# Zeros between the real products of the head of a sinkhorn-attention and MLP kernel

## The chip, the cores and the metric

One core of a Trainium2 chip runs the whole program. The metric is the device time of one execution in microseconds; the kernel before was run three times, and its median is the figure to compare with. The profile is one further execution, taken by the hardware profiler; its span runs from the first to the last instruction and is shorter than the time of a run. Engines: PE is TensorE's matmul, PEld its weight load, DVE VectorE, ACT ScalarE, POOL GpSimd, SP SyncE.

## The reference

Attention over sorted blocks (batch 4, 8 heads, sequence 768, head size 64, 8 blocks of 96), then an MLP over 3072 tokens with 512 columns inside and 2048 hidden.

```python
P = sort_net
for _ in range(5):
    P = np.exp(P - P.max(-1, keepdims=True))
    P = P / (P.sum(-1, keepdims=True) + 1e-09)
    P = P / (P.sum(-2, keepdims=True) + 1e-09)
k_sorted = einsum('bhij,bhjcd->bhicd', P, k_blocks)   # v alike
scores = scale * q_b @ k_sb.T
attn = softmax(scores)          # within each block
x = (attn @ v_sb)               # then as (tokens, 512)
h = x @ w_in
out = (h * cos(h)) @ w_out
```

## The kernel before

The order of every engine's instructions is the order of the Python code: the scheduling is manual, and each engine works through its own queue in order. The pools only hand out buffers, and waits are set between the instructions that share one.

The work is cut into eight pieces n of 384 tokens (four blocks, u = 0 to 3, of one batch half). For a piece: `qk` makes scores in PSUM (`sc`), takes the maximum and subtracts it on VectorE (`mx`, `s`); `expo` makes the exponentials on ScalarE (`p_buf`); `p_transpose` turns them on TensorE (`pps`) and copies them to `pT`; `av` multiplies with the sorted values `vS` and normalizes on VectorE (`r`, `xn`); `x_transpose` turns the result (`xps`) into `xT`. `moe_up` makes h (line 553), its cosine (ScalarE, line 557) and the product `gg` (VectorE, line 560); `moe_down` makes the output (line 570). While one piece is in its MLP, slots between its products carry the attention of the next.

The head comes before the first `moe_up`:

- Loads: `sort_net` at once; then q, k and v of the first batch on POOL's queue (lines 195 to 197), the weights later.
- `keep_warm(n)` (line 216) takes a tile `idle` of the pool `big` and issues n products of zeros, 256 columns wide, from the tile `warm`. `keep_warm(16)` is TensorE's first work.
- The normalization rounds: `product` (line 252) sums over columns on TensorE, one `sk` for each of the two groups g of batches; between them ScalarE makes `E` (line 313), VectorE `rr`, `T`, `ci` (lines 332 to 335). One round over rows first, then four rounds `it`. Rounds 1 and 2 also carry sixteen transposes of q (`qps`, line 294), whose copy to `q_turned` ScalarE makes a round later. The last round ends in `bd` (line 274), the matrices that sort k and v.
- `v_turn` (line 405) makes `bdv` from `bd`, copied by ScalarE.
- `k_sort_0` (line 349), four calls: 16, 16, 8 and 8 products `ks` of 32 columns; the first and third are cast to `kTs` by VectorE, the second and fourth by ScalarE, four casts for each call.
- `v_next` (line 605), eight calls here: each makes eight products `vs` (line 422, 64 columns) and one copy to `vS` on ScalarE. The first two take their tile from `big`, the later ones from `acc`.
- In between stand `qk(0, 0)` to `qk(0, 3)`, the four `expo`, the first two `p_transpose`, `av` and `x_transpose`. The first score needs all casts of `kTs` of this part.

PSUM: pool `big` has three buffers of two banks (1024 fp32 columns), pool `acc` two buffers of one bank (512 columns). A tile in a buffer that was used before waits until the last reader of the old tile is done.

Of the kernel before, what the change touches and what calls it, by code (L numbers as in the profile page):

```python
# [18 lines left out]
def kernel(  # L19
# [15 lines left out]
    nc = tc.nc  # L35
# [177 lines left out]
    early = const.tile([128, 1], FP32, name="early")  # L213
    nc.scalar.activation(early[:], half_pi[:], AF.Exp)

    def keep_warm(times):

        idle = big.tile([128, 256], FP32, name="idle", tag="big")
        for _ in range(times):
            nc.tensor.matmul(  # L220
                idle[:], warm[:], warm[:, :1].to_broadcast([128, 256]), start=True, stop=True)

    keep_warm(16)

# [24 lines left out]
    def along(t):  # L249
        return t[:].unsqueeze(1).to_broadcast([128, 2 * H, nb])  # L250

    def product(lhs, rhs):
        ps = acc.tile([128, nb], FP32, name="sk", tag="acc")
        nc.tensor.matmul(
            ps[:], lhs.rearrange("p x j -> p (x j)"), rhs[:], start=True, stop=True)
        return ps

    for g in range(NG):
        nc.vector.reciprocal(ci[g][:], cs[g][:])
        nc.vector.scalar_tensor_tensor(  # L260
            L[g][:], rows_of, ci[g][:], along(E[g]), op0=ALU.mult, op1=ALU.mult)
    sk = [product(L[g], maskj) for g in range(NG)]
    keep_warm(3)
    nc.vector.tensor_copy(same[:], rows_of)
    nc.vector.tensor_copy(
# [20 lines left out]
    def q_turn(n, z, pool, tag):  # L286

        ps = pool.tile([128, 2, IC, QR, blk // QR], BF16, name="qps", tag=tag)  # L290
        for e in range(2):
            for hp in range(2):
                for r in range(QR):
                    nc.tensor.transpose(
                        ps[hp * D:(hp + 1) * D, e, :, r],
                        q_rows[:, (z * 2 + e) * 2 + hp, r * D:(r + 1) * D], ident[:blk, :blk])

        def place(hp, rows):
            dst = q_of(n, hp)[rows, :QW].rearrange("d (i h c) -> d h i c", h=H2, c=blk)
            return dst[:, z * 2:z * 2 + 2], ps[rows].rearrange("d e i r p -> d e i (r p)")  # L300

        if n == 0:
            return [place(0, slice(0, 128))]
        return [place(hp, slice(hp * D, (hp + 1) * D)) for hp in range(2)]
# [6 lines left out]
    for it in range(4):  # L311
        for g in range(NG):
            nc.scalar.activation(E[g][:], T[g][:], AF.Exp, scale=ci[g][:])
        if it > 1:
            copy_on(A, *turned[0])
        sk = [product(same, E[g]) for g in range(NG)]
        if it in (1, 2):
            turned = q_turn(0, it - 1, big, "big")
        keep_warm((3, 0, 0, 3)[it])
        if it == 1:  # L320

            nc.gpsimd.tensor_copy(held[:], cs[1][:])
            for z in range(3):
                load_w_in(z)
            v_permute(slice(0, 64), D // 2, False)
        elif it == 2:
            load_w_in(3)
            load_q(1)
            for z in range(4):
                load_w_out(z)  # L330
        for g in range(NG):
            nc.vector.reciprocal(rr[g][:], sk[g][:])
            nc.vector.tensor_tensor_reduce(
                T[g][:], E[g][:], rr[g][:], 1.0, 1e-9, ALU.mult, ALU.add, cs[g][:])
            nc.vector.reciprocal(ci[g][:], cs[g][:])
            if it == 3:
                spread(g)
# [10 lines left out]

    def k_sort_0(ih, t0, nt, eng, pool, tag):

        ps = pool.tile([128, nt, 2 * MH], FP32, name="ks", tag=tag)
        for t in range(nt):
            k_products(ps, t, t0 + t, slice(64, 128),
                       bds[0][64:, H:, ih * IC:(ih + 1) * IC])
        ms, ts = slice(ih * MH, (ih + 1) * MH), slice(t0, t0 + nt)
        psv = ps.rearrange("p t (e m) -> p e m t", e=2)
        for hp in range(2):
            for x in range(2):
                copy_on(eng, kT[0][hp * D:(hp + 1) * D, hp + x, ms, ts],
                        psv[x * D:(x + 1) * D, hp])  # L360

    def k_sort_1(t0, eng, pool, tag):
        ps = pool.tile([128, 8, 2 * NB], FP32, name="ks", tag=tag)
        for t in range(8):
            k_products(ps, t, t0 + t, slice(0, 128),
                       bds[0][:, :H].rearrange("p x i -> p (x i)"))
        copy_on(eng, kT[1][:, ::2, :, t0:t0 + 8], ps.rearrange("p t (e m) -> p e m t", e=2))

    def k_sort_g(t0, eng, pool, tag):
        ps = pool.tile([128, 4, 4 * NB], FP32, name="ks", tag=tag)  # L370
        for t in range(4):
            k_products(ps, t, t0 + t, slice(0, 128), bds[1].rearrange("p x i -> p (x i)"),
                       pair)
        copy_on(
            eng, kT2[:, ::2, :, :, t0:t0 + 4].rearrange("p e b m t -> p b e m t"),
            ps.rearrange("p t (b e m) -> p b e m t", b=2, e=2))
# [26 lines left out]
    bdv = const.tile([128, 2 * H, nb], BF16, name="bdv")  # L403

    def v_turn():
        ps = big.tile([128, 128], FP32, name="bdp", tag="big")
        for r in (0, 64):
            nc.tensor.matmul(
                ps[r:r + 64], ident[:, 64 - r:128 - r], bds[0].rearrange("p x i -> p (x i)"),
                start=True, stop=True)  # L410
        nc.scalar.copy(bdv.rearrange("p x i -> p (x i)"), ps[:])
# [2 lines left out]
        return vperm[:, d * blk:d * blk + 128] if permuted else vv[:, d]  # L414

    def v_sort_b(b, d0, nd, eng, pool, tag):
        ps = pool.tile([128, nd, 2 * NB], FP32, name="vs", tag=tag)


        rows, xs = slice(0, 64 + b * 64), slice((1 - b) * H, (2 - b) * H)  # L420
        for t in range(nd):
            nc.tensor.matmul(  # L422
                ps[:, t], v_cols(d0 + t, b == 1 or d0 + t >= D // 2)[rows],
                bdv[rows, xs].rearrange("p x i -> p (x i)"), start=True, stop=True)
        copy_on(
            eng, vS[0][:, b * 2 * NB:(b + 1) * 2 * NB, d0:d0 + nd],
            ps[:blk].rearrange("p t n -> p n t"))

    def v_sort_g(d0, nd, eng, pool, tag):
        ps = pool.tile([128, nd, 4 * NB], FP32, name="vs", tag=tag)  # L430
        for t in range(nd):
            nc.tensor.matmul(  # L432
                ps[:, t], v_cols(d0 + t, True), bds[1].rearrange("p x i -> p (x i)"),
                start=True, stop=True)
        copy_on(eng, vS[1][:, :, d0:d0 + nd], ps[:blk].rearrange("p t n -> p n t"))
# [9 lines left out]

    def qk_part(n, u, part, pool, tag):
        w = len(part)
        sc = pool.tile([128, w, 512], FP32, name="sc", tag=tag)
        for h2 in range(H2):
            for e, hp in enumerate(part):  # L450
                scores(sc[:, e, h2 * blk:(h2 + 1) * blk], n, u, h2, hp)
        scv = sc[:blk, :, :H2 * blk].rearrange("p e (h c) -> p e h c", c=blk)
        mx = small.tile([blk, w, H2], FP32, name="mx", tag="mx")
        nc.vector.reduce_max(mx[:], scv, axis=AX.X)  # L454
        nc.vector.tensor_tensor(  # L455
            s_t[n, u][:, part[0]:part[0] + w], scv, mx.to_broadcast([blk, w, H2, blk]),
            op=ALU.subtract)
# [40 lines left out]

    def p_transpose(n, u, eng, pool, tag):
        p = pb.pop((n, u))  # L500
        ps = pool.tile([128, 2 * H2, 128], BF16, name="pps", tag=tag)
        for a in range(2 * H2):
            nc.tensor.transpose(ps[:blk, a, :blk], p[:, a, :blk], ident[:blk, :blk])  # L503
        copy_on(eng, pT[n, u][:blk], ps[:blk, :, :blk])

    def av(n, u, on_pe=False):
        g, b2, ih = where(n)
        if n not in xT:
            xT[n] = xtp.tile([128, KC, TC], BF16, name="xT", tag="xT")
        a = big.tile([128, 2, 512], FP32, name="av", tag="big")  # L510
        pt = pT.pop((n, u)).rearrange("p a c -> p (a c)")
        for hp in range(2):
            for h2 in range(H2):
# [20 lines left out]

    def x_transpose(n, u, eng, pool, tag):
        xn = xn_t.pop((n, u))
        ps = pool.tile([128, KC, blk], BF16, name="xps", tag=tag)

        turn = order[:] if n < NQ else ident[:blk, :blk]
        for h2 in range(H2):  # L540
# [4 lines left out]

    def up(n, fp, lo=0, hi=TC):

        h = big.tile([128, 2, 512], FP32, name="h", tag="big")
        w = hi - lo
        for f2 in range(2):  # L550
            f = fp * 2 + f2
# [12 lines left out]

    def down(n, ts, half, stores, mid=()):
        if half == 0:
            out_ps[ts] = acc.tile([128, Dm], FP32, name="o", tag="acc")
        o = out_ps[ts]
        for f in range(half * FC // 2, (half + 1) * FC // 2):
            nc.tensor.matmul(  # L570
# [40 lines left out]
    k_sort_0(0, 16, 16, A, *C)  # L611
    k_sort_0(0, 32, 8, V, *B)
    k_sort_0(0, 40, 8, A, *C)
    v_next(A, *B)
    v_next(A, *B)
    qk(0, 0)
    v_next()
    qk(0, 1)
# [3 lines left out]
    v_next()  # L622
    expo(0, 0, True)
    v_next()
    p_transpose(0, 0, A, *B)
    expo(0, 1, True)
    v_next()
    qk(0, 3)
    v_next()
    p_transpose(0, 1, A, *B)  # L630
    av(0, 0, True)
    av(0, 1, True)
    expo(0, 2, True)
    expo(0, 3, True)
    x_transpose(0, 0, V, *C)
    x_transpose(0, 1, V, *C)

    load(vbuf, 64, vin_d[1])

# [126 lines left out]

    ts, w = TC // 128 - 1, Dm // 2
    for z, (eng, dma) in enumerate(((A, nc.scalar), (V, nc.sync))):
        o = acc.tile([128, w], FP32, name="o", tag="acc")
        for f in range(FC):  # L770
            nc.tensor.matmul(  # L771
                o[:], gt[7, f // 2][:, f % 2, ts * 128:(ts + 1) * 128],
# [34 lines left out]
```

## Time and profile before

| | us |
|---|---|
| median of three runs | 251.34 |
| lowest, highest run | 249.9, 251.37 |
| span of the profiled execution | 248.0 |
| TensorE busy in it | 231.1 (93%) |
| VectorE busy | 175.8 (71%) |
| ScalarE busy | 157.3 (63%) |
| POOL busy | 88.2 (36%) |
| mean granted clock of TensorE | 0.945 |

A page of the profile gives busy time by engine, the span in 40 slices of 6.2 us (a digit is the busy share in tenths; PEclk is the clock that TensorE was granted, in tenths of full speed), DMA queues, the chain of waits followed back from the last instruction, and the costliest groups of instructions. Views of the trace give the same for a chosen stretch, or the instructions in order of time. In a timeline a line reads: start, duration (merged over xN instructions), engine, line, operation, out<-in, sizes, and in brackets the idle time of the engine before it and what ended that.

### The profile page before, as it was taken

How to read it: one execution, taken by the hardware profiler on the slowest of the kernel's cores; microseconds unless marked ns; L12 is line 12 of the kernel's file. 1: busy time of each engine (PE TensorE's matmuls, PEld its weight loads, DVE VectorE, ACT ScalarE, POOL GpSimd, SP SyncE). 2: the span in 40 equal slices, each digit the busy share in tenths (PEclk: the TensorE clock that was granted, in tenths of full speed). 3: DMA queues.
4: the chain of work that ended last, by engine and by line, in shares of the span. 5: the costliest groups of instructions: out<-in, count | busy, mean ns of one | idle time of the engine just before them, and what ended most of it. 6: DMA issues, size and time to landing. Idle time of an engine off the chain costs nothing.

```text
span 248.0 us, 5329 instructions
## 1 busy us (share of the span) xinstructions
PE 231.1 (93%) x2131; PEld 148.7 (60%) x2151; DVE 175.8 (71%) x322; ACT 157.3 (63%) x224; POOL 88.2 (36%) x104
## 2 busy tenths in 40 slices
PE   7887798878999999999999999999999999979994
PEld 5776696745566656665666556655565556435543
DVE  5579558897478876688568997898789759524710
ACT  4467846676568975789568866684667456634710
POOL 6369990799879707110353500800000000000000
PEclk9655569999999999999999999999999999999999
DMA  5999999895997058846897978937651650371012
GB/s 55 232 193 174 197 201 231 134 213 105 181 233 130 6 137 110 136 110 148 172 102 134 59 184 151 158 39 181 153 110 32 176 114 0 97 119 42 0 43 86
DMA packets 69001, 31.49 MB, mean 127 GB/s; under 512 B 57840, under 2 KB 64496, under 8 KB 68720
## 3 DMA queue, kind: packets, MB, share of 16 engines
q0 software_dynamic: 24048, 13.64, 40.8%
q1 hardware_dynamic: 43408, 15.28, 27.2%
q10 hardware_dynamic: 1520, 2.24, 2.8%
q8 instruction: 17, 0.28, 0.5%
q14 instruction: 8, 0.07, 0.1%
HBM read 27.27 MB, written 6.29 MB: 135 GB/s over the span
## 4 chain that ended last, share of the span: by engine, by line
PE 75%; DVE 10%; ACT 6%; DMA 5%; issue 2%; ACTq 0%; DVEq 0%; SPq 0%
PE h L553 32%; PE o L570 24%; PE sc L399 3%; PE av L516 3%; DMA vperm<-p_buf 2%; PE pps L503 2%; ACT p_buf L479 2%; DVE kTs L282 2%; PE ks L346 2%; PE vs L432 1%; DVE gg L560 1%; PE o L771 1%; DVE xn L525 1%; PE vs L422 1%; PE xps L541 1%
## 5 line engine op out<-in xcount | busy, mean ns | idle before, releaser
L553 PE MATMUL h<-xT,w_in_t 128*128 128x384 bf16 (+1 forms) x576 | 93.3, 313 | 2.1 <-DVE gg L560 0.8
L570 PE MATMUL o<-w_out_t,gg 128*128 128x512 bf16 x348 | 84.0, 379 | 1.6 <-DVE s L455 0.5
L557 ACT ACTIVATE c<-h,half_pi 128x768 f32<-128x768 f32 (+1 forms) x72 | 59.7, 830 | 36.2 <-PE h L553 33.9
L560 DVE TENSOR_TENSOR gg<-c,h 128x768 bf16<-128x768 f32 (+1 forms) x72 | 61.3, 859 | 25.2 <-ACT c L557 25.1
L553 PEld LDWEIGHTS <-w_in_t 128*128 128x128 bf16 x576 | 53.8, 100 | 29.7 <-issue 2.9
L570 PEld LDWEIGHTS <-gg 128*128 128x128 bf16 x368 | 33.6, 98 | 33.6 <-DVE s L455 0.7
L454 DVE TENSOR_REDUCE mx<-sc 96x4 f32<-96x384 f32 (+1 forms) x43 | 31.9, 741 | 3.2 <-PE sc L399 2.3
L455 DVE TENSOR_TENSOR s<-sc,mx 96x384 f32<-96x384 f32 (+1 forms) x43 | 32.2, 749 | 2.3
L177 POOL COPY vperm<-kv 64x1536 bf16<-64x1536 bf16 (+1 forms) x10 | 28.2, 2841 | 6.2 <-DMA kv<-in_v_dram 5.2
L479 ACT ACTIVATE p_buf<-s 96x768 bf16<-96x768 f32 x32 | 27.6, 894 | 2.4 <-ACT o_s L280 1.0
L280 ACT COPY o_s<-o 128x512 f32<-128x512 f32 (+1 forms) x18 | 10.3, 573 | 25.0 <-PE o L570 23.8
L525 DVE TENSOR_TENSOR xn<-av,r 96x512 bf16<-96x512 f32 x32 | 22.0, 686 | 1.1
L280 ACT CAST kTs<-ks 128x512 bf16<-128x512 f32 (+2 forms) x31 | 14.1, 456 | 6.2 <-PE ks L346 6.0
L134 POOL DMA_DIRECT2D kv<-in_q_dram x24 | 16.0, 675 | 3.1 <-DMA kv<-in_v_dram 2.2
L399 PE MATMUL sc<-kTs,q_turned 128*128 128x96 bf16 x224 | 16.1, 206 | 0.9 <-DVE s L455 0.7
L523 DVE RECIPROCAL r<-av 96x8 f32<-96x8 f32 x32 | 6.4, 199 | 14.7 <-PE av L516 14.6
L399 PEld LDWEIGHTS <-q_turned 128*128 128x128 bf16 x224 | 12.8, 98 | 4.8 <-DVE s L455 1.3
L282 DVE COPY o_s<-o 128x512 f32<-128x512 f32 (+1 forms) x7 | 4.5, 647 | 12.1 <-PE o L771 8.6
L557 ACT ACT_TABLE_LOAD x8 | 10.3, 1283 | 0.9 <-ACT o_s L280 0.7
L134 POOL DMA_DIRECT2D q_mem<-in_q_dram x16 | 10.6, 675 | 0.3 <-issue 0.3
L280 ACT CAST pair<-vs 96x512 bf16<-96x512 f32 (+1 forms) x12 | 8.7, 728 | 2.5 <-PE vs L432 2.0
L516 PEld LDWEIGHTS <-pT 96*128 96x128 bf16 (+1 forms) x160 | 7.8, 106 | 3.4 <-issue 1.2
(96 smaller groups left out, 212.8 us busy)
## 6 DMA issues: line engine op xcount, KB each, us to landing
out_dram<-o_s SPq DMA_DIRECT2D x15, 256.0 KB, 2.6
w_in_t<-in_moe_w_in_dram POOLq DMA_DIRECT2D x4, 512.0 KB, 10.6
w_out_t<-in_moe_w_out_dram POOLq DMA_DIRECT2D x4, 512.0 KB, 12.9
out_dram<-o_s ACTq DMA_DIRECT2D x8, 256.0 KB, 2.5
kv<-in_k_dram POOLq DMA_DIRECT2D x2, 768.0 KB, 13.3
kv<-in_v_dram POOLq DMA_DIRECT2D x2, 768.0 KB, 16.5
pair<-in_k_dram POOLq DMA_DIRECT2D x2, 768.0 KB, 11.5
kv<-in_v_dram POOLq DMA_DIRECT2D x6, 256.0 KB, 6.2
```

Source lines behind the costliest of these rows:

```text
L134: nc.gpsimd.dma_start(out=q_heads[:, i, :, e], in_=src[:, ih * IC + i, :, e])
L177: nc.gpsimd.tensor_copy(dst, src)
L280: eng.copy(dst, src)
L399: nc.tensor.matmul(out, q_of(n, hp)[:, x:x + 128], keys_of(n, u, h2, hp), start=True, stop=True)
L454: nc.vector.reduce_max(mx[:], scv, axis=AX.X)
L455: nc.vector.tensor_tensor(s_t[n, u][:, part[0]:part[0] + w], scv, mx.to_broadcast([blk, w, H2, blk]), op=ALU.subtract)
L479: nc.scalar.activation(dst, src, AF.Exp, scale=scale)
L525: nc.vector.tensor_tensor(xn.rearrange("p h e d -> p e h d"), avv[:, :, :, :D], r.to_broadcast([blk, 2, H2, D]), op=ALU.mult)
L553: nc.tensor.matmul(h[:, f2, :w], w_in_t[:, kk, f * 128:(f + 1) * 128], xT[n][:, kk, lo:hi], start=(kk == 0), stop=(kk == KC - 1))
L557: nc.scalar.activation(c[:, :, :w], h[:, :, :w], AF.Sin, bias=half_pi[:, 0:1])
L560: nc.vector.tensor_tensor(gt[n, fp][:, :, lo:hi], c[:, :, :w], h[:, :, :w], op=ALU.mult)
L570: nc.tensor.matmul(o[:], gt[n, f // 2][:, f % 2, ts * 128:(ts + 1) * 128], w_out_t[:, f, :], start=(f == 0), stop=(f == FC - 1))
```

## The change

A helper `psum` replaces the direct calls of the two PSUM pools. It takes the whole buffer as one flat tile (1024 or 512 fp32 columns), issues into its first 256 columns as many zeros as `fill` has asked for since the last tile, and hands out the view of the shape that was asked for. `fill_behind(n)` issues n zeros into columns 512 to 767, the second bank, of the tile handed out last. The zeros are those of `keep_warm`: the 128x128 tile `warm` as weights, one of its columns repeated 256 times as data. Every zero is a weight load and a product.

Fifty zeros are new: five ahead of the second `sk` of a pair (one in the first pair, then two, one and one in rounds 1, 2 and 3), three more in `keep_warm` of round 0 and one more in that of round 3, and 41 by `fill` and `fill_behind` around the first piece's attention.

```diff
+    pending, last = [0], [None]
+
+    def zeros_into(dst, times):
         for _ in range(times):
             nc.tensor.matmul(
-                idle[:], warm[:], warm[:, :1].to_broadcast([128, 256]), start=True, stop=True)
+                dst, warm[:], warm[:, :1].to_broadcast([128, 256]), start=True, stop=True)
+
+    def fill(times):
+        pending[0] += times
+
+    def fill_behind(times):
+        zeros_into(last[0][:, 512:768], times)
+
+    def psum(pool, shape, name, tag, dtype=FP32):
+        flat = pool.tile([128, 1024 if tag == "big" else 512], FP32, name=name, tag=tag)
+        zeros_into(flat[:, :256], pending[0])
+        pending[0], last[0] = 0, flat
...
-    def product(lhs, rhs):
-        ps = acc.tile([128, nb], FP32, name="sk", tag="acc")
+    def product(lhs, rhs, zeros=0):
+        fill(zeros)
+        ps = psum(acc, [128, nb], "sk", "acc")
...
-    sk = [product(L[g], maskj) for g in range(NG)]
+    sk = [product(L[g], maskj, g) for g in range(NG)]
...
-        sk = [product(same, E[g]) for g in range(NG)]
+        sk = [product(same, E[g], g * (0, 2, 1, 1)[it]) for g in range(NG)]
...
-        keep_warm((3, 0, 0, 3)[it])
+        keep_warm((6, 0, 0, 4)[it])
...
     k_sort_0(0, 40, 8, A, *C)
+    fill(4)
     v_next(A, *B)
+    fill_behind(5)
     v_next(A, *B)
+    fill_behind(4)
     qk(0, 0)
...
     v_next()
+    fill(7)
     p_transpose(0, 0, A, *B)
     expo(0, 1, True)
     v_next()
     qk(0, 3)
     v_next()
+    fill(5)
     p_transpose(0, 1, A, *B)
+    fill(3)
     av(0, 0, True)
+    fill(3)
     av(0, 1, True)
     expo(0, 2, True)
     expo(0, 3, True)
+    fill(3)
     x_transpose(0, 0, V, *C)
+    fill(3)
     x_transpose(0, 1, V, *C)
+    fill(4)
```

The last `fill(4)` goes ahead of the first h. The other calls of the pools (`qps`, `ks`, `bdp`, `vs`, `sc`, `pps`, `av`, `xps`, `h`, `o`) are the same tiles taken through `psum`, with no zeros of their own.

More of the change, by code (lines that the diff above doesn't have):

```diff
@@ L214, with keep_warm @@
     nc.scalar.activation(early[:], half_pi[:], AF.Exp)
-    def keep_warm(times):
-        idle = big.tile([128, 256], FP32, name="idle", tag="big")
+    pending, last = [0], [None]
+    def zeros_into(dst, times):
         for _ in range(times):
             nc.tensor.matmul(
-                idle[:], warm[:], warm[:, :1].to_broadcast([128, 256]), start=True, stop=True)
+                dst, warm[:], warm[:, :1].to_broadcast([128, 256]), start=True, stop=True)
[7 more added lines that the diff above has]
+        pending[0], last[0] = 0, flat
+        x = flat[:] if dtype == FP32 else flat[:].bitcast(dtype)
+        dims = " ".join("abcde"[:len(shape) - 1])
+        return x[:, :math.prod(shape[1:])].rearrange(
+            f"p ({dims}) -> p {dims}", **dict(zip("abcde", shape[1:])))
+    def keep_warm(times):
+        zeros_into(psum(big, [128, 256], "idle", "big")[:], times)
     keep_warm(16)
@@ L286, in q_turn @@
     def q_turn(n, z, pool, tag):
-        ps = pool.tile([128, 2, IC, QR, blk // QR], BF16, name="qps", tag=tag)
+        ps = psum(pool, [128, 2, IC, QR, blk // QR], "qps", tag, BF16)
         for e in range(2):
@@ L349, in k_sort_0 @@
     def k_sort_0(ih, t0, nt, eng, pool, tag):
-        ps = pool.tile([128, nt, 2 * MH], FP32, name="ks", tag=tag)
+        ps = psum(pool, [128, nt, 2 * MH], "ks", tag)
         for t in range(nt):
@@ L362, in k_sort_1 @@
     def k_sort_1(t0, eng, pool, tag):
-        ps = pool.tile([128, 8, 2 * NB], FP32, name="ks", tag=tag)
+        ps = psum(pool, [128, 8, 2 * NB], "ks", tag)
         for t in range(8):
@@ L369, in k_sort_g @@
     def k_sort_g(t0, eng, pool, tag):
-        ps = pool.tile([128, 4, 4 * NB], FP32, name="ks", tag=tag)
+        ps = psum(pool, [128, 4, 4 * NB], "ks", tag)
         for t in range(4):
@@ L405, in v_turn @@
     def v_turn():
-        ps = big.tile([128, 128], FP32, name="bdp", tag="big")
+        ps = psum(big, [128, 128], "bdp", "big")
         for r in (0, 64):
@@ L416, in v_sort_b @@
     def v_sort_b(b, d0, nd, eng, pool, tag):
-        ps = pool.tile([128, nd, 2 * NB], FP32, name="vs", tag=tag)
+        ps = psum(pool, [128, nd, 2 * NB], "vs", tag)
         rows, xs = slice(0, 64 + b * 64), slice((1 - b) * H, (2 - b) * H)
@@ L429, in v_sort_g @@
     def v_sort_g(d0, nd, eng, pool, tag):
-        ps = pool.tile([128, nd, 4 * NB], FP32, name="vs", tag=tag)
+        ps = psum(pool, [128, nd, 4 * NB], "vs", tag)
         for t in range(nd):
@@ L447, in qk_part @@
         w = len(part)
-        sc = pool.tile([128, w, 512], FP32, name="sc", tag=tag)
+        sc = psum(pool, [128, w, 512], "sc", tag)
         for h2 in range(H2):
@@ L500, in p_transpose @@
         p = pb.pop((n, u))
-        ps = pool.tile([128, 2 * H2, 128], BF16, name="pps", tag=tag)
+        ps = psum(pool, [128, 2 * H2, 128], "pps", tag, BF16)
         for a in range(2 * H2):
@@ L509, in av @@
             xT[n] = xtp.tile([128, KC, TC], BF16, name="xT", tag="xT")
-        a = big.tile([128, 2, 512], FP32, name="av", tag="big")
+        a = psum(big, [128, 2, 512], "av", "big")
         pt = pT.pop((n, u)).rearrange("p a c -> p (a c)")
@@ L536, in x_transpose @@
         xn = xn_t.pop((n, u))
-        ps = pool.tile([128, KC, blk], BF16, name="xps", tag=tag)
+        ps = psum(pool, [128, KC, blk], "xps", tag, BF16)
         turn = order[:] if n < NQ else ident[:blk, :blk]
@@ L546, in up @@
     def up(n, fp, lo=0, hi=TC):
-        h = big.tile([128, 2, 512], FP32, name="h", tag="big")
+        h = psum(big, [128, 2, 512], "h", "big")
         w = hi - lo
@@ L566, in down @@
         if half == 0:
-            out_ps[ts] = acc.tile([128, Dm], FP32, name="o", tag="acc")
+            out_ps[ts] = psum(acc, [128, Dm], "o", "acc")
         o = out_ps[ts]
@@ L768 @@
     for z, (eng, dma) in enumerate(((A, nc.scalar), (V, nc.sync))):
-        o = acc.tile([128, w], FP32, name="o", tag="acc")
+        o = psum(acc, [128, w], "o", "acc")
         for f in range(FC):
```

## The prediction

> **What bounds the kernel now.** I read the span in slices first, then cut the head along the changes of the granted clock, then read the timelines of TensorE, ScalarE and VectorE in the head beside the chain of waits.
>
> ```profile
> PE   7887798878999999999999999999999999979994
> PEclk9655569999999999999999999999999999999999
> ```
>
> From slice 7 on (37 us) TensorE is nine tenths busy at the full clock; the chain of waits gives the products into h 32% and those into o 24%. Before that stands the head, where the clock is about half. The zeros lie there alone, so only the head can change.
>
> ```profile
> 1.06:4.48 3.42, 3.42 (x16) 2.22 (x16) 2.13 (x8) 2.06 (x6) 3.42 (x8) 1.00 0.26 18
> 4.48:7.89 3.41, 2.66 (x17) 1.77 (x16) 2.20 (x18) 1.03 (x4) 0.56 (x3) 0.98 1.33 215
> 7.89:11.30 3.41, 3.19 (x39) 2.89 (x39) 1.98 (x16) 1.75 (x5) 2.07 (x3) 0.50 1.08 227
> ...
> 28.37:31.78 3.41, 2.96 (x25) 2.73 (x25) 0.93 (x4) 1.90 (x3) 3.26 (x6) 0.50 1.24 201
> 31.78:35.19 3.41, 3.41 (x41) 3.24 (x40) 1.60 (x5) 1.16 (x2) 3.30 (x5) 0.51 1.19 196
> ...
> 243.41:246.83 3.42, 1.44 (x14) 1.04 (x11) 1.00 0.26 90
> 246.83:248.00 1.17, 0.00 (x0) 0.00 (x0) 0.00 (x0) 0.00 (x0) 0.00 (x0) 1.00 0.00 0
> ```
>
> These are stretches of 3.41 us: time, then busy time and count of PE, PEld, DVE, ACT, POOL, then clock, DMA share, GB/s (the row of 243.41 is the one for line 771's products alone). The clock falls at 7.89 and comes back at 35.19, which is eight such stretches later, so I read it as decided once per stretch.
>
> ```profile
> 1.04 3.53 PE L220 MATMUL idle<-warm 128*128 128x256 bf16 x16 [1.04 <-DVE warm L209]
> ...
> 5.24 0.49 PE L220 MATMUL idle<-warm 128*128 128x256 bf16 x3
> ...
> 14.64 0.95 PE L422 MATMUL vs<-bdv,kv 64*128 64x64 bf16 x8
> 16.17 0.93 PE L422 MATMUL vs<-bdv,kv 64*128 64x64 bf16 x8 [0.59 <-DVE kTs L282]
> 17.49 0.56 PE L394 MATMUL sc<-kTs,q_turned 64*96 64x96 bf16 x8 [0.39 <-DVE kTs L282]
> ```
>
> The first sixteen zeros take 3.42/16 = 0.213 us each (half clock, though the column says 1.00), three later ones 0.49 with their tail; the last 32 products of the kernel, also 256 columns, take 3.51/32 = 0.11 us at full clock. That is 0.83 and 0.42 ns a column. Counting columns, not busy time: the stretch to 4.48 was full, and the clock rose. The next held six zeros, 0.66 us or 0.2 of it, and the clock fell, though TensorE shows 2.66 us busy. The stretch from 243.41 holds 1.44/3.42 = 0.42 and the clock stays at 1.00 behind it. So staying up needs a share between 0.2 and 0.42. At half clock the stretch from 28.37 counts about 0.8 and did not raise it, the next about 0.95 (it is without a gap) and did.
>
> ```profile
> 14.39 2.60 ACT L280 CAST kTs<-ks 64x256 bf16<-64x256 f32 x8 [0.70 <-PE ks L346]
> 17.02 1.07 ACT L280 CAST vS<-vs 96x512 bf16<-96x512 f32 x2
> ```
>
> ```profile
> 14.39 2.95 DVE L282 CAST kTs<-ks 64x256 bf16<-64x256 f32 x8
> 18.08 0.95 DVE L454 TENSOR_REDUCE mx<-sc 96x8 f32<-96x768 f32 x1 [0.74 <-PE sc L394]
> ...
> 28.79 0.36 DVE L282 COPY xT<-xps 128x384 bf16<-128x384 bf16 x1 [0.33 <-PE xps L541]
> ```
>
> The first scores (17.49) wait for VectorE's casts of the keys. From their end at 18.05 to the first h at 29.20 VectorE has four pairs mx and s (1.90 each, back to back to 25.90), two pairs r and xn (1.81), two copies xT. From 29.20 to 34.51 TensorE alone paces: three groups of h at 1.28 to 1.44 and two transposes pps at 0.64 on the chain.
>
> **The change part by part.** Fifty zeros: five between the two sk products of a round, four more in the calls of keep_warm, 41 ahead of or behind later products. Nothing is taken out and no DMA or queue moves; ScalarE, VectorE and POOL keep their order. Pool slots stay as they are (big 3, acc 2), so a zero that opens a tile waits for the slot that the product waited for anyway.
>
> *Does the clock hold?* At 0.11 us each: 4.48 to 7.89 gets 1+3+6 zeros, 1.1 us, 0.32. To 11.30: four zeros 0.44, 32 transposes at 0.49 per sixteen (full clock, the chain at 40.68), 1.42, 0.42. To 14.72: eight zeros 0.88, 48 ks of 32 columns 0.64, bdp 0.11, 0.48. To 18.13: five zeros 0.55 and sixteen vs of 64 columns 0.43, 0.29 (why so few is the next paragraph). Later stretches hold 0.6 or more. All lie between 0.2 and 0.42 or above; the two low ones at 0.32 and 0.29 are nearer the middle than an end. I take it that the clock holds, narrowly, and keep both ends.
>
> The Trainium skill ("TensorE: Matmul & The Clock Gate", the table "Why this matters for your kernels") wants only idle gaps above about 3 us avoided, and by it the sum would have no gain, only the added wait and the zeros' own time. The stretch from 4.48 contradicts it here: no gap in it is above 0.51 us and the clock fell.
>
> *The wait that the change adds.* The five zeros behind the first v_next and the four behind the second go into the second bank of that v_next's tile. In the built program the five wait for ScalarE's copy vS of that same tile, and the four for the second copy vS. TensorE's queue runs in order, so the second vs, all scores and everything else stand behind. ScalarE reaches the first vS copy only after its eight casts of the keys. In the timeline of before that is 17.02, each copy 0.58 (the pair takes 1.07 overlapped), while TensorE, done with the first vs at 15.59, waited there only 0.59 us, for one of VectorE's casts.
>
> *Sum, clock held.* Rounds of sk: two sk products take 0.40 at full clock instead of 0.59, and sixteen qps 0.49 instead of 0.79; ScalarE's copy q_turned (0.78, between the rounds) hides part. The chain E, sk, rr, T, ci then has bd at 12.49 instead of 13.01: -0.5. Zeros between the sk of a round sit in gaps of 0.2 to 0.5 where the second E isn't ready; without that cover they would be 0.55. ks issues at 30 ns each at both clocks (48 in 1.46; later 16 in 0.49), so ScalarE's casts end at 16.99-0.54 = 16.45. Then vS 0.60, zeros 5 x 0.11, eight vs 0.40 (full clock, from 73.80 on), vS 0.60, zeros 4 x 0.11 and hand-overs 0.15: the scores begin at 19.1 and end at 19.45 instead of 18.05. Without the wait they would begin behind VectorE's casts, 17.35-0.5, and end at 17.2; so it costs 2.25.
>
> Behind that VectorE is next: 4 x 1.90, then r and xn 1.81, the last xps and xT 0.85: 10.3 us, first h at 29.75, +0.55. The other 28 zeros are hidden: seven before pps(0,0) run from 21.35 while ScalarE makes p_buf to 22.4, five before pps(0,1) end at 24.45 before p_buf at 24.8, and those before av, xps and h lie under VectorE's xn and xT. Were that cover gone they would cost up to 28 x 0.11 = 3.1. Then h runs at full clock: three groups at 0.8 and two pps at 0.5 (eight took 0.54 to 0.56 later), 3.4 instead of 5.3. The third cosine starts at 33.15 instead of 34.51: -1.4. From here the two agree. Nothing fixed takes it back: by the landings the last quarter of w_in is there at 27.1, w_out at 40.5, the next k at 43.3, v at 47.0, first needed (shifted) at 36, 50, 52 and 66.
>
> The profiled execution has a span of 248.0; I forecast 246.6 for it. The runs lie 1.9 to 3.4 above that span, which the edit leaves alone: 251.34-1.4 = **249.9 us**.
>
> **Rivals.** *The clock falls at 18.13* (share 0.29 too little). Everything to then is as above; four zeros and the first scores run at half clock, 19.45 becomes 20.05, the queue is then full and the clock comes back by 24.95. -1.4+0.6 = -0.8: 250.5. For it: 0.29 lies only 0.09 above a share that failed.
>
> *The clock falls at 7.89 as before*: slower. It decides if 0.32 is under the needed share. No gain in the sk rounds, and the added wait at half clock: casts end at 17.2 (one more zero ahead, 0.21), vS 0.6, zeros 1.07, vs 0.93, vS 0.6, zeros 0.85, scores 0.56: they end at 21.85, +3.8. The VectorE path of 10.3 gives h at 32.15, by then at full clock since zeros have filled a stretch; third cosine at 35.6, +1.1: 252.4. If no stretch fills until 35, the later zeros at 0.21 add up to 3: 255.4. For it: 0.2 failed, 0.32 is little; against: 0.42 of plain products held.
>
> *The stretches lie elsewhere in the timed runs.* The three runs differ by 1.47 us, and the rise at 35.19 needed a full stretch; one that starts at another place rises a stretch earlier or later, worth about 1.4 to the kernel before. The zeros make the new one less dependent on it: 1.4+1.4, 248.5. Against: the profiled windows begin just where the zeros do. The Trainium skill (same page, "What's actually happening") calls the window free-running, not reset at a kernel's start, which is what this rival needs; one trace can't show it.
>
> *Zeros don't count*, so the change does not do what it says: as the second rival with no rise, 255. Against: sixteen of them are all that preceded the rise at 4.48.
>
> **How the numbers follow.** Chances: forecast 0.36, fall at 18.13 0.17, fall at 7.89 0.25, stretches elsewhere 0.14, zeros not counted 0.08. A measurement of this kernel tells about 1%, 2.5 us, from no change. Faster than 248.8: 0.3 of the forecast's cases (0.11; the hand-sums may be off by a microsecond) and two thirds of the fourth (0.09): 0.20. Slower than 253.9: 0.45 of the third (0.11), nearly all of the last (0.08): 0.19. Within: 0.61. The range 247.6 to 253.6 leaves out about 0.05 below and 0.14 above. The forecast's own range is 248.3 to 250.9.
>
> **What would show it.** Right: full clock across 7.89 to 35; TensorE idle ahead of line 220's zeros into vs with ScalarE's copy vS as the releaser; first scores near 19.1; h near 29.7. Wrong: scores before 18 (the wait does not bind), or 0.21 us zeros after 8 us (the clock fell), or VectorE idle between the pairs mx and s.

## The result and the profile after

Over eleven runs each, the changed kernel takes 253.5 us (252.37 to 256.15) and the kernel before 251.34 (249.9 to 252.68): a ratio of 1.0121, interval 1.009 to 1.0152. The change makes the kernel slower by 2 to 4 us; 249.9 was forecast. A ratio here and below leaves out the runs that lie over 1.5% above the fastest of their kernel (one each of `a_no9_order`, `f_no9` and the kernel before, four of `f_dense`), while the medians include them. The two profiled executions lie at opposite ends: 249.9 is the run that the profile of before shows (span 248.0), and 255.74 the run that this one shows (span 254.0). The medians differ by 2.2 us, so 3.8 of the 6.0 between the spans is the choice of runs, and what the two traces suggest has to be tested on medians.

The head of the changed kernel on TensorE's timeline (start, duration, engine, line; the zeros are line 220):

```profile
18.32 1.23 PE L220 MATMUL vs<-warm 128*128 128x256 bf16 x5 [1.04 <-ACT vS L302]
...
21.07 1.01 PE L220 MATMUL vs<-warm 128*128 128x256 bf16 x4 [0.68 <-ACT vS L302]
22.01 0.55 PE L416 MATMUL sc<-kTs,q_turned 64*96 64x96 bf16 x8
...
25.38 1.68 PE L220 MATMUL pps<-warm 128*128 128x256 bf16 x7
...
34.25 0.61 PE L220 MATMUL h<-warm 128*128 128x256 bf16 x4
34.86 0.82 PE L575 MATMUL h<-xT,w_in_t 128*128 128x192 bf16 x8
```

The reader is to see three things. TensorE stands twice ahead of zeros into `vs`, with ScalarE's copy vS named as the releaser. The first scores come at 22.01 instead of 17.49, and the first h at 34.86 instead of 29.20. And the zeros take 0.21 us each at first (a row's time holds a tail; the seven take 1.68, the four 1.01), while the four at 34.25 take 0.61 with the tail, 0.11 each: up to there the clock was at half for the whole head. The clock's own row does not say so:

```profile
PEclk9999999999999999999999999999999999999999
```

The row starts with the first change that is on record; here that is the rise at 33.7, and what lies ahead of it is printed as full. Why it rose so late stays open. Counted back in steps of 3.41 us, a border of stretches lies at 3.0, in the middle of the sixteen first zeros (1.04 to 4.6), so that neither stretch beside it was full. But in `a_rounds` (below), which has the same products in the rounds, a border lies at 2.89, and the clock rose at 6.30, behind a stretch that was hardly fuller (0.71 of it streamed, 0.69 of the one from 3.0 here; the count is explained with `f_dense`). The mean granted clock of a run tells the same: 0.959 to 0.966 where the clock rose early and fell again (six of the eleven runs, median 252.93), 0.998 to 1.0 where it rose only at the end of the head (five, 254.99). For the kernel before, over the 88 runs beside the experiments, that is 250.74 (55 runs) and 251.26 (33). The change loses in both cases.

ScalarE and VectorE in the same stretch of the changed kernel:

```profile
15.07 2.59 ACT L302 CAST kTs<-ks 64x256 bf16<-64x256 f32 x8 [0.69 <-PE ks L368]
17.68 0.59 ACT L302 CAST vS<-vs 96x512 bf16<-96x512 f32 x1
20.43 0.59 ACT L302 CAST vS<-vs 96x512 bf16<-96x512 f32 x1 [2.16 <-PE vs L444]
```

```profile
14.75 2.81 DVE L361 COPY order<-ident 96x96 bf16<-96x96 bf16 x1
17.48 2.95 DVE L304 CAST kTs<-ks 64x256 bf16<-64x256 f32 x8
22.61 0.95 DVE L476 TENSOR_REDUCE mx<-sc 96x8 f32<-96x768 f32 x1 [2.18 <-PE sc L416]
```

ScalarE reaches the first vS only behind its eight casts, and TensorE's five zeros wait for it. VectorE shows something that the forecast had not looked at: its copy `order`, 0.23 us at 14.25 in the profile of before, takes 2.81 here. It is a second suspect for the late scores, since the casts of the keys stand behind it.

### The profile page after: what moved, and what is told of

It is laid out like the page before. It is cut to its first block, busy times and chain, and to the rows that moved or that the text cites. A ratio compares the mean times of both kernels' runs of the same rounds, so it can differ in the third digit from the quotient of the medians.

```text
span 254.0 us, 5447 instructions
## 1 busy us (share of the span) xinstructions
PE 238.4 (94%) x2201; PEld 153.3 (60%) x2201; DVE 178.9 (70%) x322; ACT 157.5 (62%) x224; POOL 88.4 (35%) x104
## 4 chain that ended last, share of the span: by engine, by line
PE 76%; DMA 8%; DVE 6%; ACT 6%; issue 2%; ACTq 0%; DVEq 0%; SPq 0%
PE h L575 30%; PE o L592 21%; DMA vperm<-p_buf 4%; DMA pT<-p_buf 4%; PE sc L421 3%; PE idle L220 3%; PE av L538 2%; PE ks L368 2%; PE vs L444 2%; DVE gg L582 2%; ACT kTs L302 2%; PE pps L525 2%; PE sk L276 1%; DVE s L477 1%; PE o L803 1%
## 5 line engine op out<-in xcount | busy, mean ns | idle before, releaser
L575 PE MATMUL h<-xT,w_in_t 128*128 128x384 bf16 (+1 forms) x576 | 91.4, 308 | 2.2 <-DVE o_s L304 1.1
L592 PE MATMUL o<-w_out_t,gg 128*128 128x512 bf16 x368 | 87.2, 379 | 0.5 <-DVE s L477 0.5
L575 PEld LDWEIGHTS <-w_in_t 128*128 128x128 bf16 x576 | 52.4, 98 | 29.4 <-issue 2.0
L302 ACT COPY o_s<-o 128x512 f32<-128x512 f32 (+1 forms) x18 | 10.3, 573 | 25.0 <-PE o L592 23.7
L220 PEld LDWEIGHTS <-warm 128*128 128x128 bf16 x75 | 10.2, 149 | 5.5 <-issue 1.7
L302 ACT CAST vS<-vs 96x512 bf16<-96x512 f32 x16 | 9.1, 579 | 5.0 <-PE vs L444 5.0
L579 ACT ACT_TABLE_LOAD x8 | 10.3, 1283 | 0.9 <-DVE xn L547 0.7
## 6 DMA issues: line engine op xcount, KB each, us to landing
w_in_t<-in_moe_w_in_dram POOLq DMA_DIRECT2D x4, 512.0 KB, 10.3
```

Of the source, the lines that this page charges most:

```text
L220: nc.tensor.matmul(dst, warm[:], warm[:, :1].to_broadcast([128, 256]), start=True, stop=True)
L302: eng.copy(dst, src)
L575: nc.tensor.matmul(h[:, f2, :w], w_in_t[:, kk, f * 128:(f + 1) * 128], xT[n][:, kk, lo:hi], start=(kk == 0), stop=(kk == KC - 1))
L579: nc.scalar.activation(c[:, :, :w], h[:, :, :w], AF.Sin, bias=half_pi[:, 0:1])
L592: nc.tensor.matmul(o[:], gt[n, f // 2][:, f % 2, ts * 128:(ts + 1) * 128], w_out_t[:, f, :], start=(f == 0), stop=(f == FC - 1))
```

## The experiments

Medians are in us, with the number of runs; each ratio is against the kernel before, run beside it on the same chip. Its medians were 250.93 (beside the first four kernels), 251.03 (`a_front9`, `a_wait1`, `a_rounds`, `a_fills`), 250.88 (the `f_` kernels) and 251.11 (`a_nine`, `a_fills2`).

**The two suspects.** In `a_order` VectorE's copy goes to POOL, ahead of POOL's own copies; `a_no9` drops the nine zeros; `a_no9_order` does both; `b_order` moves the copy in the kernel before.

```diff
-    fill_behind(5)
     v_next(A, *B)
-    fill_behind(4)
```
```diff
+            nc.gpsimd.tensor_copy(
+                order.rearrange("k (p r) -> k p r", r=QR),
+                ident[:blk, :blk].rearrange("k (r p) -> k p r", r=QR))
             v_permute(slice(0, 64), D // 2, False)
...
-    nc.vector.tensor_copy(
-        order.rearrange("k (p r) -> k p r", r=QR),
-        ident[:blk, :blk].rearrange("k (r p) -> k p r", r=QR))
```

> The changed kernel with VectorE's small copy of `order` moved to POOL, ahead of POOL's copies of v. In the profile of the changed kernel that copy started on VectorE 0.08 us after POOL's first v copy and took 2.81 us instead of 0.23, and VectorE's casts of the keys ended at 20.4 instead of 17.35. Theory block (this copy is the loss): casts end near 17.7, the first score moves from 22.0 to 20.5 or earlier, time 253.5 less about 1.5 to 2 = 251.5 to 252. Theory wait (TensorE's stand behind ScalarE's copies vS, and the nine zeros themselves, end later than the casts anyway): first score stays at 21.5 to 22.0, time 253.0 to 253.5.

> The changed kernel without the nine zeros behind the first two v_next, and so without the wait for ScalarE's copies vS. Theory wait: idle time of 1.04 and 0.68 and nine zeros at 0.21 go, the first score moves from 22.0 to 18.4, time about 250. Theory block: the first score can't come before VectorE's casts, 20.4, so it gains 1.5 and the time is about 252. Forecast's theory that the zeros' own time costs nothing and only the wait costs: 253.5 less 1.7 = 251.8 with the first score at 20.3.

> Both: no nine zeros, and the copy of `order` on POOL. Theory that wait and block stand one under the other: only this one brings the first score to about 18.1, 3.9 earlier, and the time to 249.8 to 250.3. If the block alone or the wait alone is the loss, it is no faster than the one of the two single edits that removes it.

> The kernel before with the copy of `order` on POOL. In its profile that copy ran 14.25 to 14.48, 0.16 us before POOL's v copy at 14.64, so an execution whose rounds end 0.2 later would be blocked for 2.8. Theory block: the runs above 251.5 go, median about 250.5. Rival (the spread of the runs is from the clock or from the DMA): no change, 251.3.

| kernel | median, runs | ratio | interval |
|---|---|---|---|
| a_order | 254.38, 4 | 1.0126 | 1.0069 to 1.0184 |
| a_no9 | 251.01, 10 | 1.0016 | 0.9991 to 1.0041 |
| a_no9_order | 252.13, 10 | 1.0028 | 0.9991 to 1.0064 |
| b_order | 251.08, 10 | 0.9999 | 0.9973 to 1.0024 |

VectorE's timeline of `a_order`:

```profile
14.95 2.95 DVE L304 CAST kTs<-ks 64x256 bf16<-64x256 f32 x8
22.83 0.95 DVE L475 TENSOR_REDUCE mx<-sc 96x8 f32<-96x768 f32 x1 [4.93 <-PE sc L415]
```

The casts end 2.5 us earlier and VectorE then idles 4.93 instead of 2.18, waiting for the same late scores: the long copy lay under TensorE's stand and cost nothing that can be measured. Nor is `a_no9_order`, expected at 249.8 to 250.3, faster than `a_no9`. TensorE's timeline of `a_no9`:

```profile
17.49 0.56 PE L416 MATMUL sc<-kTs,q_turned 64*96 64x96 bf16 x8 [0.33 <-ACT vS L302]
...
29.14 0.82 PE L575 MATMUL h<-xT,w_in_t 128*128 128x192 bf16 x8
```

Without the nine zeros the first scores are at the 17.49 of before and the loss is gone, although the other 41 zeros are all there.

**The zeros or the wait?** `a_front9` keeps all fifty zeros, but the nine go ahead of the second v_next, into a tile whose buffer is free, so that none of them waits for a copy vS. `a_wait1` keeps both stands with one zero each. `a_nine` has only the nine, where the change has them, and none of the 41.

```diff
-    fill_behind(5)
+    fill(9)
     v_next(A, *B)
-    fill_behind(4)
```
```diff
-    fill_behind(5)
+    fill_behind(1)
     v_next(A, *B)
-    fill_behind(4)
+    fill_behind(1)
```

> The changed kernel with the nine zeros moved ahead of the second v_next, where they wait only for what that product waits for anyway. Same number of zeros, no stand behind ScalarE's two copies vS. Without the nine: 251.0; with them behind: 253.5. Theory wait: the stand of 1.04 and 0.68 us and the second copy vS between are the loss, the time is 251.0 to 251.5. Theory own time: nine zeros at 0.21 us in TensorE's queue are the loss, 253.0 or more. Half each: about 252.2, first score near 20.3.

> The changed kernel with one zero in place of five and one in place of four behind the first two v_next: both waits stay, seven zeros (1.5 us at half clock) go. Theory wait: still 253 or more. Theory own time: 251.3. Half each: 252.0 to 252.4, first score near 20.5 where the changed kernel had 22.0.

> Of the fifty zeros only the nine behind the first two v_next. Theory (the stand behind ScalarE's two copies vS is the loss, the other 41 zeros are worth nothing): first scores at 21 to 22.3, 2 to 3 us longer than before. Rival (the 41 take part in the loss, or carry some of it): 1 us or less over before, or over 3.5.

| kernel | median, runs | ratio | interval |
|---|---|---|---|
| a_front9 | 250.57, 10 | 1.0002 | 0.9969 to 1.0036 |
| a_wait1 | 252.65, 7 | 1.0081 | 1.0048 to 1.0114 |
| a_nine | 254.32, 4 | 1.0152 | 1.0101 to 1.0202 |

TensorE in `a_front9`, in `a_wait1`, and in `a_nine`:

```profile
16.69 2.10 PE L220 MATMUL vs<-warm 128*128 128x256 bf16 x9
...
19.23 0.31 PE L416 MATMUL sc<-kTs,q_turned 64*96 64x96 bf16 x1
```
```profile
18.20 0.37 PE L220 MATMUL vs<-warm 128*128 128x256 bf16 x1 [1.03 <-ACT vS L302]
...
20.10 0.37 PE L220 MATMUL vs<-warm 128*128 128x256 bf16 x1 [0.67 <-ACT vS L302]
20.40 0.55 PE L416 MATMUL sc<-kTs,q_turned 64*96 64x96 bf16 x8
```
```profile
17.88 1.23 PE L220 MATMUL vs<-warm 128*128 128x256 bf16 x5 [2.10 <-ACT vS L302]
...
21.57 0.56 PE L416 MATMUL sc<-kTs,q_turned 64*96 64x96 bf16 x8
```

In `a_front9` the same nine zeros run at the same half clock while ScalarE and VectorE cast, and wait for neither. They do push the head: the first scores are at 19.23 and the first h at 31.20, against 17.49 and 29.14 in `a_no9`. But at the end nothing that can be measured is left of it. With the stands and only two zeros the first scores are at 20.40, 2.9 late, and about two thirds of the loss are there. That lies between the two theories (253 or more, 251.3), so the seven other zeros, 1.5 us in the queue behind the waits, are part of the loss. With nothing but the nine behind vS it is there whole. The loss is the order of the queue: vs, copy, zeros, vs, copy, zeros, scores run one after another instead of side by side. What the stands would cost at full clock no run shows.

**The other 41 alone.** `a_rounds` keeps only the nine zeros of the rounds and of keep_warm, `a_fills` only the 32 later ones without a wait of their own; `a_fills2` is that kernel again. The edit of `a_fills`:

```diff
-    sk = [product(L[g], maskj, g) for g in range(NG)]
+    sk = [product(L[g], maskj) for g in range(NG)]
...
-        sk = [product(same, E[g], g * (0, 2, 1, 1)[it]) for g in range(NG)]
+        sk = [product(same, E[g]) for g in range(NG)]
...
-        keep_warm((6, 0, 0, 4)[it])
+        keep_warm((3, 0, 0, 3)[it])
...
-    fill_behind(5)
     v_next(A, *B)
-    fill_behind(4)
```

> Only the nine zeros of the sk rounds and keep_warm; the 41 later ones left out. If they hold the clock up behind an early rise (the forecast's step), the granted clock of runs with an early rise is above 0.952 and the time 0.5 under before, 250.4. If the clock falls all the same and the zeros only stand ahead of sk products, 251.0 to 251.4.

> Only the 32 later zeros that have no wait of their own; the nine of the rounds and the nine behind v_next left out. They bring the clock's rise forward from 35 to 23 to 27 us but stand in TensorE's queue at 0.21 us until then. Theory that both cancel: 250.7 to 251.2. Theory that the zeros' own time outweighs: 251.5 or more. Theory that the clock outweighs: 250.3 or less.

> The 32 later zeros without a wait of their own, for a second time (the first time 254.29 over four runs). Theory (these zeros are hidden; the first time was four unlucky runs): 250.5 to 252. Rival (they cost 2 to 3 us by themselves, and the nine zeros of the rounds take it back): 253.5 to 255 again.

`a_rounds`: 251.23 over 10 runs, 1.0015 (0.9986 to 1.0043). `a_fills`: 254.29 over 4 runs, 1.013 (1.0075 to 1.0185); `a_fills2`: 252.91 over 7, 1.0098 (1.0058 to 1.0138). In the trace of `a_rounds` the clock was full from 6.30 to 13.13, and the first scores came 0.58 us earlier than before:

```profile
16.91 0.56 PE L416 MATMUL sc<-kTs,q_turned 64*96 64x96 bf16 x8
```

So the forecast's gain in the rounds is there (the first h is at 28.58 instead of 29.20), and no time comes of it.

`a_fills` lies well above the 250.7 to 251.2 of hidden zeros, and `a_fills2` between its two theories. In the trace of `a_fills2` the head is not where the time is lost. Of each stage's start there and in before, the first product into o is at 49.3 and at 52.0, the second stage of o at 82.1 and 83.8, but the h after it at 100.1 and 98.3. TensorE's timeline of `a_fills2` in that stretch:

```profile
92.89 0.43 PE L538 MATMUL av<-vS,pT 96*128 96x65 bf16 x8 [1.88 <-DMA pT<-p_buf]
...
93.39 3.52 PE L592 MATMUL o<-w_out_t,gg 128*128 128x512 bf16 x8
```

The lead of the head is lost at a transfer, and then once more at the clock. TensorE waits 1.88 us for the transpose pT, which takes 4.38 in the chain of waits here and 2.60 in the kernel before. Behind that thin stretch (0.37 of it streamed) the clock fell: it is at 0.50 from 93.48 to 96.90, where eight products into o take 3.52 us instead of the 1.89 of the eight at 88.87. Together that is 3.5 us, the whole way from 1.7 ahead to 1.8 behind. The other trace, `a_fills`, has no such fall on record and reaches that h at 99.5. The chain of `a_fills2` also goes through the keys' swap (kTs<-kTs, two copies of 192 KB on SP's queue, 9.32 us from 62.97), which the chain of the kernel before passes by. Why the kernel with all 41 (`a_no9`) comes out at 251.0 with much the same head is not settled: its chain has the swap too (8.91), but its transpose pT at 89.27 took 2.61.

**Can the lead of an early head be kept?** In `a_no9` the scores behind the swap wait for it:

```profile
71.94 0.33 PE L421 MATMUL sc<-kTs,q_turned 128*128 128x96 bf16 x4 [0.45 <-DMA kTs<-kTs]
```

POOL's six loads of v (256 KB each) move beside it. In the `f_` kernels they are issued only once the swap has landed, in a slot behind it:

```diff
-    for z in range(6):
-        load_pair(vbuf, vin_d, z * CD // 6, (z + 1) * CD // 6)
+    def late_v():
+        nc.gpsimd.tensor_copy(held[:], kT[1][:, 1, 0, :1])
+        for z in range(6):
+            load_pair(vbuf, vin_d, z * CD // 6, (z + 1) * CD // 6)
...
-                  (av, 1, 2, True), (p_transpose, 1, 3, A, *B), (k_swap, kT[1])],
+                  (av, 1, 2, True), (p_transpose, 1, 3, A, *B), (k_swap, kT[1]), (late_v,)],
```

> The changed kernel without the nine zeros behind the first two v_next, and with POOL's six loads of v issued only after the keys' swap by DMA has landed. Theory (the swap, slowed to 8.9 us by the loads beside it, is the floor under an early head): the swap takes some 3 us, no score waits for it, and the head's 3 us come through in part: 1.5 to 2.3 us under the same kernel with the loads where they were, 248.7 to 249.5 against 251.0. Rival (the gain is lost later anyway, in the transposes by DMA): unchanged, 250.7 to 251.3.

> The changed kernel with the nine zeros ahead of the second v_next, and with the six loads of v behind the swap. The head is up to 2 us later than in the kernel without the nine, so the theory gives somewhat less: 249.0 to 250 against 250.6 with the loads where they were. Rival: 250.4 to 250.9, unchanged.

> The kernel before, with nothing changed but the six loads of v behind the swap. Its own head reaches the scores behind the swap just after the swap lands, so the theory allows it next to nothing: 0 to -0.5 us. If it gains 1.5 us or more, the swap bound it too and the place of the loads is worth that much by itself, without any zeros.

| kernel | median, runs | ratio | interval |
|---|---|---|---|
| f_no9 | 252.27, 10 | 1.0048 | 1.0017 to 1.0079 |
| f_front9 | 252.30, 10 | 1.0062 | 1.0030 to 1.0094 |
| f_before | 251.70, 10 | 1.0025 | 0.9998 to 1.0052 |

The theory fell as a remedy: none of the three is faster than its pair with the loads where they were, and two are slower than the kernel before. The swap did come down (the median of its two copies is 4.3 us in `f_no9`, 8.7 in `a_no9`) and no score waits for it. But what it freed is waited for one stage later. SP's queue in `f_no9`, then TensorE's waits between 55 and 101 us (total, times, longest):

```profile
83.25 3.61 SPq L147 DMA_TRANSPOSE q_turned<-kv  x2
86.97 3.95 SPq L512 DMA_TRANSPOSE pT<-p_buf  x2
```
```profile
PE av L538 <- DMA pT<-p_buf: 2.7, 1, 2.7
```

In `a_no9` SP had the transposes q_turned behind it at 79.3 (they were issued at 75.63), and the first pT went at 84.70. The late v loads hold up POOL's loads of q (from 73.86 instead of 63.83), those the transposes q_turned, and these stand on SP's queue ahead of pT. Part of the later pT is the head itself, whose first product into o is 1.2 us later in this execution. In the trace of `f_front9` the clock fell as well in that place (0.50 from 92.39 to 95.81).

**Can the clock be held through the head, and is it worth it?** `f_dense` is `f_front9` with 24 more zeros in the rounds (the expectation says 26).

```diff
-    sk = [product(L[g], maskj, g) for g in range(NG)]
+    sk = [product(L[g], maskj, 3 * g) for g in range(NG)]
...
-        sk = [product(same, E[g], g * (0, 2, 1, 1)[it]) for g in range(NG)]
+        sk = [product(same, E[g], g * (0, 4, 4, 4)[it]) for g in range(NG)]
...
-        keep_warm((6, 0, 0, 4)[it])
+        keep_warm((10, 3, 3, 8)[it])
```

> As the kernel with nine zeros ahead of the second v_next and the loads of v behind the swap, with 26 more zeros in the rounds (two more ahead of the first second sk, two to four per round, four to three more in each keep_warm). Theory (the clock holds once the streamed share of every stretch passes 0.41): zeros of 0.11 us each and full clock from the first rise through the head to 20 us, first h 1 to 2 us earlier in executions where the clock rises, time equal to the kernel with fewer zeros or up to 1 us less. Rival (the share is not what decides): the clock falls again within two stretches of the rise, the added zeros stand at 0.21 us in the rounds, and the time is 1 to 3 us longer.

Its stretches of 3.41 us from the recorded rise on (time, then busy time and count of PE, PEld, DVE, ACT, POOL, granted clock, DMA share, GB/s):

```profile
4.15:7.56 3.41, 3.05 (x26) 2.24 (x25) 2.43 (x19) 1.06 (x5) 0.53 (x1) 1.00 1.19 172
7.56:10.98 3.42, 3.42 (x58) 3.06 (x56) 2.10 (x19) 1.91 (x6) 2.43 (x4) 1.00 1.04 219
10.98:14.39 3.41, 3.41 (x71) 2.96 (x69) 2.40 (x14) 1.70 (x5) 0.00 (x0) 1.00 0.94 196
14.39:17.80 3.41, 1.87 (x18) 1.47 (x17) 2.30 (x7) 2.55 (x8) 1.42 (x1) 1.00 1.22 202
17.80:21.22 3.42, 3.42 (x45) 2.88 (x43) 1.15 (x2) 1.25 (x3) 3.42 (x2) 0.50 1.24 207
```

The count behind the shares is that of the forecast, streamed columns: 0.42 ns each at full clock, 0.83 at half, fp32 columns twice. Products that stream at the same time count once: q's transposes do so in pairs (sixteen of 96 columns start within 0.35 us from 40.61 on in the kernel before, where one after another they would need 0.6). By it the first four stretches hold 0.49, 0.71, 0.65 and 0.31; the clock stays up behind the first three and falls behind the fourth. The same two stretches of `a_front9`, with the rounds of the change:

```profile
5.37:8.78 3.41, 3.07 (x26) 2.08 (x27) 2.02 (x18) 1.20 (x4) 1.01 (x3) 1.00 1.31 235
8.78:12.19 3.41, 3.41 (x42) 3.11 (x42) 1.74 (x14) 2.29 (x6) 1.42 (x2) 0.50 1.06 223
```

There the first holds 0.39, and the clock falls. This fits that the streamed share decides, and that zeros can hold the clock until they run out. The count gives no sharp limit, though. A share moves by up to 0.05 when products are placed by the ends of their records instead of the starts. And a stretch of `f_no9` with a long wait for pT in it holds 0.38, and the clock stayed up:

```profile
87.52:90.94 3.42, 1.49 (x10) 0.70 (x8) 1.42 (x2) 1.54 (x3) 3.42 (x2) 1.00 1.13 131
90.94:94.35 3.41, 2.43 (x25) 1.43 (x27) 1.06 (x3) 1.27 (x2) 3.41 (x2) 1.00 0.77 198
```

Whether a held clock is worth anything stays open. The ratio of `f_dense` is 1.0028 (0.9992 to 1.0063), median 252.79 over ten runs. The six runs with the early rise (mean clock 0.972 to 0.985) took 252.17 to 260.72 and the other four 251.48 to 252.59. Only two of those six are in the ratio, and what made the other four, the profiled one among them, so long is not shown. The first h, expected 1 to 2 us earlier, is at 32.46 against 31.20 in `a_front9`. One row of that profile at least names a next limit, on TensorE's timeline:

```profile
16.37 0.89 PE L444 MATMUL vs<-bdv,kv 64*128 64x64 bf16 x8 [1.54 <-DMA kv<-in_v_dram]
```

A head at full clock comes to the first v before v has landed. In this execution v was late (POOL's copy of it starts at 16.38, at 14.64 in before), but `a_rounds` has the same wait, 1.12 us until 15.17.

No kernel of these beats the kernel before by what can be measured; `a_front9` (250.57 against 251.03) equals it.

## Why the prediction was wrong

The forecast was 1.4 us faster, and the kernel became 2 to 4 us slower. That 253.5 lies just inside the range up to 253.6 is owed to the rivals that the range had to cover, not to the mechanism that was chosen.

- *"I take it that the clock holds, narrowly."* The step that failed. It rested on one share that held (0.42) and one that fell (0.2), and put the limit under 0.29. Later stretches close it in: behind 0.41 the clock stayed up (`a_rounds`, `f_no9`), behind 0.39 (`a_front9`), 0.38 (`a_no9`), 0.37 and 0.31 it fell, and 0.38 held once (`f_no9`, from 87.52). The forecast's own 0.32 and 0.29 were well under. Its 0.42 for the stretch to 11.30 was too high as well: it took 0.49 us with a tail for sixteen transposes, and by their starts, 0.35, the stretch holds about 0.33. In no profiled execution with the change's zeros was the clock held to the end of the head; in the changed kernel's own it was at half up to 33.7.
- *The stretches from 4.48 on.* The forecast laid the new stretches on the grid of before. The rise stands at 4.15, 5.37, 5.94 and 6.30 in other traces, and at 33.7 in that of the changed kernel. The Trainium skill ("TensorE: Matmul & The Clock Gate", "What's actually happening") calls the window free-running, not reset at the kernel's start, and these traces agree. By the same section of the Trainium skill what is issued after the first 3.4 us or so runs at full clock; the changed kernel's 33.7 us contradicts that. How full a stretch has to be for a rise is not settled: 0.71 was enough in `a_rounds` (2.89 to 6.30), 0.92 was not in the changed kernel (26.85 to 30.26).
- *The added wait.* Its place was right, to the row: both stands, ScalarE's copies, scores behind them. Its price was put at 2.25 us at full clock; the first scores came 4.5 late in the changed kernel and 4.1 in `a_nine`, at half clock. The rival "the clock falls as before" had the scores end at 21.85 (22.56 was seen) and named both outcomes: 252.4 where a stretch fills early, 255.4 where none does. The runs gave 252.93 and 254.99, though no trace shows the first kind. It had a chance of 0.25 and should have been the forecast; 0.36 for a clock that needed two shares in an unmeasured gap was too much.
- *"10.3 us, first h at 29.75".* The path behind the scores was put too short: in before it takes 11.15 (18.05 to 29.20), in `a_nine` 11.14, both at half clock, and in `a_no9`, at full clock from 23.0 on, 11.09.
- *"Zeros between the sk of a round sit in gaps" and "the other 28 zeros are hidden".* At the end hidden in effect: `a_nine` without the 41 is as slow as the change, `a_no9` with them is as fast as before. But `a_fills` and `a_fills2`, with 32 of them alone, are about 1% slower. In the head they are not hidden at half clock: from the first scores to the first h the changed kernel takes 12.85 us with the 28 zeros and `a_nine` 11.70 without. The gain of 0.5 in the rounds comes where the clock holds through them (0.58 in `a_rounds`), and no time is won by it.
- *"Nothing fixed takes it back."* Wrong too, by an omission, and enough by itself to take the forecast's gain: the landings listed were w_in, w_out, k and v, not the keys' swap or the transposes. `a_no9` reaches the first o at 49.2 instead of 52.0 and ends level. A lead of 2.8 us is worth nothing here, while a delay is passed on: 4.1 us at the first h of `a_nine`, 3.2 at its end.
- *What would show it wrong: "0.21 us zeros after 8 us".* That is what the trace showed. No long wait was needed for it: in the stretch 5.37 to 8.78 of `a_front9` TensorE waited at no point more than 0.2 us, and the clock fell behind it all the same.

## What to carry to other kernels

Filler that keeps a clock up has to go where its engine's queue would stand anyway, into a buffer that is already free: the same nine products cost nothing that could be measured ahead of a tile and 3 us behind one, because in an in-order queue a filler that waits for a reader makes everything behind it wait too. Before a forecast counts on a clock that holds, find in the trace a share that held and a share that fell and see whether the new stretches lie outside the gap between them; inside it, take the sum at half clock as the likelier. Count what streams from one start to the next, not from rows with their tails. And a gain in an early stage counts only if the transfers of the next stages can follow, so list every transfer that lies between it and the end.

## What the runs showed of the hardware

- What keeps the clock up is how much of a 3.41-us stretch streams, with a limit near 0.4: behind 0.41 it stayed up in two kernels, behind six stretches of 0.35 to 0.39 it fell (one each of `a_front9`, `a_no9`, `a_rounds`, `a_fills2`, `f_no9` and `f_front9`), behind two of 0.38 (`f_no9`, from 87.52) and 0.39 (before, the last products) it stayed up.
- A wait in mid-kernel can cost twice: behind 1.88 us for a transpose the clock of `a_fills2` fell for one stretch, and eight products took 3.52 us instead of 1.89. In `f_front9` it fell at the same place.
- VectorE's bf16 copy of 96 columns took 0.23 us at 14.25, ahead of POOL's copy (14.64), and 2.81 at 14.75, just after POOL's copy had begun (14.67). The Trainium skill ("SBUF — State Buffer", "SBUF: two separate sides") describes a port pair that VectorE's 2-port modes and POOL hold by turns for a whole instruction, the other fully blocked; the trace agrees: the copy ended at 17.56, 0.1 us behind the first of POOL's two copies (5.52 for both). Moving it to POOL changed the time of neither kernel.
- The same swap of 192 KB took 7.3 to 9.3 us (median of its two copies) beside POOL's loads and 2.8 to 4.3 when these came later.
